# A long convolution's second half: joined loads, a filter that goes through DRAM, and loads five groups ahead

## The chip, the cores and the metric

The kernel runs on one core of a Trainium2 chip. The metric is the device time of one execution in microseconds. Before the change it is 1845.44 us, the median of 3 runs (1845.41 to 1846.05).

## What is computed

The reference has three parts. Only the first is touched by the change; the other two take most of the time.

```python
h_filt = (np.maximum(pos_emb @ w1, 0.0) @ w2) * window      # filter, 12480 x 128
u = x * v                                                  # signal, 12480 x 128
Uf = np.fft.rfft(u, n=2*S, axis=1); Hf = np.fft.rfft(h_filt, n=2*S, axis=0)
y = np.fft.irfft(Uf * Hf[None], n=2*S, axis=1)[:, :S]; attn = x * y
# then, on 12480 tokens of 128, with d_ff = 2048
h = t @ w_in; g = P(h) / (Q(h) + 1e-06); t = g @ w_out
h = t @ w_in2; g = where(h >= 1, h, where(h <= -1, 0, (h + 1)**2 / 4)); out = g @ w_out2
```

## The kernel before

The long transform (2 blocks x 128 x 49 points) is taken apart into a transform over n1 (128 points) and one over n2 (49 points). The function `conv_transform` does this in two halves, and then the two token layers run in a software pipeline of 49 tiles.

**First half** (lines 99 to 205): 14 chunks of the 49 columns m (`CHS`: 1, 2, eleven times 4, 2). For each chunk SyncE (SP) loads positions (`pt`), `x` and `v`; GpSimd (POOL) multiplies u = x*v; TensorE (PE) makes the filter's first layer and the transform over n1 (lines 193 to 195, six matrix products for each column). ScalarE (ACT) and VectorE (DVE) move the result out of PSUM: the signal parts into the tile `so`, which ACT's queue writes to the DRAM tensor `sd`, and the filter part into `sr`, a tile that stays in SBUF with one row of the transform (k1) on each partition. `so` has two buffers, `x` and `v` have three; loads are issued four chunks ahead.

**Second half** (lines 207 to 376): 34 groups of up to four values of k1 (first one group of 1, then 31 of 4, at the end two of 2). For a group the 98 values (49 columns, real and imaginary) have to lie on partitions. So `load` and `load_u` fetch `gt` (matrix of the transform over n2), `rr` (filter rows, four transfers out of `sr`, each from one partition of SBUF to 98) and `ru` (signal rows out of `sd`), all on SP's queue; `load_inv` fetches `gi`, the inverse matrix, at the step that runs. Then:

- `R`: transform of the filter rows on PE (line 244), split into a high and a low part by ACT (line 88) and DVE (line 89);
- `AB`: product with the second layer's weights on PE (lines 255 to 258), copied by ACT (line 260);
- `U`: transform of the signal on PE (line 269) into the PSUM tile `up`, which has one buffer;
- `M`: the spectral product, four operations on DVE (lines 286, 287, 289, 290) and four on POOL;
- `Tr` and `Inv`: transposes (line 306) and inverse transform (line 322) on PE with ACT copies, and the store of `co` into the DRAM tensor `cd` on ACT's queue.

Step s of the loop works on several groups at once: loads for s+3, AB for s+1, U and M for s, R for s+2, Tr for s-2, Inv for s-3. Beside it each step decodes a part of the layers' weights, which come as 64-bit floats: `fill` takes one of 32 fillers, each a load (line 57, two buffers), six operations on DVE (lines 68 to 71, 73, 74) and one or two on POOL, every second time one on ACT. The order is written out by hand, and every engine and SP's queue run in that order.

**After it** the layers' pipeline starts when the last part of `cd` has been written; its tiles load two columns of `cd` each (line 491).

Of the kernel before, what the change touches and what calls it, by code (L numbers as in the profile page):

```python
# [44 lines left out]
def decode_steps(nc, pool, src, n, dst):  # L45
    """float64 bits (src, int32 pairs low/high) to float32 in dst(), rounded to nearest:
    one closure per instruction."""
    e = {}

    def tile_(name, dt):  # L50
        e[name] = pool.tile([128, n], dt, name=name, tag=name, bufs=2 if name in "kt" else 1)
        return e[name]

    def load():
        e["b"] = pool.tile([128, n, 2], I32, name="b64", tag="b64", bufs=2)
        b = e["b"] if len(src.shape) == 3 else e["b"].rearrange("p (f d) t -> p f d t", f=src.shape[1])
        nc.sync.dma_start(b, src)

    def low():
        return e["b"][:, :, 0]  # L60

    def high():
        return e["b"][:, :, 1]

    ts, stt = nc.vector.tensor_scalar, nc.vector.scalar_tensor_tensor
    return [
        load,
        lambda: ts(tile_("t", I32), high(), 0x07FFFFFF, 3, op0=ALU.bitwise_and, op1=ALU.logical_shift_left),
        lambda: ts(tile_("a", I32), low(), 28, 1, op0=ALU.logical_shift_right, op1=ALU.bitwise_and),
        lambda: stt(e["t"], high(), -0x40000000, e["t"], op0=ALU.bitwise_and, op1=ALU.bitwise_or),  # L70
        lambda: stt(e["t"], low(), 29, e["t"], op0=ALU.logical_shift_right, op1=ALU.bitwise_or),
        lambda: nc.gpsimd.tensor_tensor(e["t"], e["t"], e["a"], op=ALU.add),
        lambda: ts(tile_("k", I32), high(), 27, 15, op0=ALU.logical_shift_right, op1=ALU.bitwise_and),
        lambda: stt(dst(), e["k"], 7.0, e["t"].bitcast(F32), op0=ALU.is_ge, op1=ALU.mult),
    ]


def conv_transform(tc, ident, io, cd, fillers, colsum):
    """Spectral product of u = x*v with the filter; leaves, per k1, the inverse
    transform over k2 in cd[k1, (block n2), re/im, d]."""  # L80
    nc = tc.nc
    xp, vp, posT, w1, w2, win, sgn, f1c, gc, gic = io
    with ExitStack() as ctx:
# [9 lines left out]
        sd = dram.tile([NK, N2, 2, 256], F32, name="sd")  # L93
        sr = big.tile([NK, N2, 2, D], F32, name="sr")
        w2h = big.tile([128, NB, D], F32R, name="w2h")
        w2l = big.tile([128, NB, D], F32R, name="w2l")
        rrg = pool("cv_rr", 1)

        # ---- filter MLP, u = x*v, transform over n1; block 1 takes block 0's
        # transform along, shifted by half a period  # L100
        with tc.tile_pool(name="ca", bufs=2) as ca, tc.tile_pool(name="cap", bufs=1, space=PSUM) as cap:
# [73 lines left out]
            for c in range(nch):  # L175
                if c + 4 < nch:
                    loads(c + 4)
                n = CHS[c]
                b = buf.pop(c)
                more = []  # L180
                if c + 1 < nch:
                    more += [lambda: parts(c + 1, 0)]
                if c + 2 < nch:
                    products(c + 2)
                    more += [lambda: mlp(c + 2)]
                if c + 1 < nch:
                    more += [lambda: parts(c + 1, 1)]
                so = ca.tile([NK, mx, 2, 256], F32, name="so", tag="so")
                for j in range(n):
                    sp = cap.tile([128, 2, 512], F32, name="sp", tag="sp", bufs=3)  # L190
                    for r in range(2):
                        o = sp[:, r, 0:SIG]
                        nc.tensor.matmul(o, f1h[:, r], b["h"][:, j], start=True, stop=False)
                        nc.tensor.matmul(o, f1l[:, r], b["h"][:, j], start=False, stop=False)
                        nc.tensor.matmul(o, f1h[:, r], b["l"][:, j], start=False, stop=True)
                    nc.scalar.copy(so[:, j, :, 0:128], sp[:, :, 0:128])
                    nc.scalar.copy(sr[:, first[c] + j], sp[:, :, 128:256])
                    nc.vector.scalar_tensor_tensor(so[:, j, :, 128:256], so[:, j, :, 0:128], sgt,
                                                   sp[:, :, 256:384], op0=ALU.mult, op1=ALU.add)
                    if more:  # L200
                        more.pop(0)()
                for fn in more:
                    fn()
                nc.scalar.dma_start(sd[:, first[c]:first[c] + n], so[:, 0:n])
            split(w2h, w2l, w2b)

        # ---- per k1: transform over n2, product, inverse transform over k2
# [4 lines left out]
        cdr = cd.rearrange("k (b m) r d -> (m r) k b d", b=NB)  # L212
        groups = [(NK, 1)] + [(4 * i, 4) for i in range(NK // 4 - 1)] + [(NK - 4, 2), (NK - 2, 2)]
        ng = len(groups)
        G = [dict() for _ in groups]

        def load(g):
            k0, n = groups[g]
            e = G[g]
            row = k0 % NK  # L220
            v, nb, m = ("n", 1, 1) if n == 1 else ("", 4, 4)
            e["rr"] = rrg.tile([SL, m, D], F32, name="rr", tag="rr" + v, bufs=nb)[:, 0:n]
            e["gt"] = rrg.tile([SL, m, SL], F32, name="gt", tag="gt" + v, bufs=nb)[:, 0:n]
            nc.sync.dma_start(e["gt"], gc[:, k0:k0 + n])
            for i in range(n):
                nc.sync.dma_start(e["rr"][:, i], sr[row + i:row + i + 1].rearrange("k m r s -> k (m r) s"))  # L226

        def load_u(g):
            k0, n = groups[g]
            row = k0 % NK  # L230
            G[g]["ru"] = (big if n == 1 else pre).tile([SL, n if n == 1 else 4, 256], F32, name="ru", tag=f"ru{min(n, 2)}", bufs=1 if n == 1 else 4)
            nc.sync.dma_start(G[g]["ru"][:, 0:n], sdr[:, row:row + n])

        def load_inv(g):
            k0, n = groups[g]
            G[g]["gi"] = (big if n == 1 else pre).tile([SL, n if n == 1 else 4, SL], F32, name="gi", tag=f"gi{min(n, 2)}", bufs=1 if n == 1 else 4)
            nc.sync.dma_start(G[g]["gi"][:, 0:n], gic[:, k0:k0 + n])

        def R(g):
# [3 lines left out]
            for i in range(n):  # L243
                nc.tensor.matmul(rp[:, i], e["rr"][:, i], e["gt"][:, i], start=True, stop=True)
# [17 lines left out]
        def U(g):  # L262
# [4 lines left out]
            for i in range(n):  # L267
                for b in range(NB):
                    nc.tensor.matmul(uv[:, i, b * SL:(b + 1) * SL], e["ru"][:, i, b * D:(b + 1) * D],
# [40 lines left out]
        def Inv(g, h):  # L310
# [13 lines left out]
            if h + 2 == n:  # L324
                for b in range(NB):
                    (nc.scalar if g < ng - TQ else nc.sync).dma_start(cdr[:, k0:k0 + n, b], e["co"][:, 0:n, b * D:(b + 1) * D])

        fills = fillers(pool("cv_fill", 1))
        late = []

        def fill(i):
            nonlocal late
            for fn in late:
                fn()
            late = []
            if i + 1 < len(fills):
                fills[i + 1][0]()
            if i < len(fills):
                for fn in fills[i][1:6]:
                    fn()  # L340
                late = fills[i][6:]

        for g in range(3):
            load(g)
        for g in range(3):
            load_u(g)
        fills[0][0]()
# [5 lines left out]
        for s in range(-2, ng + 3):  # L353
            if 3 <= s + 3 < ng:
                load(s + 3)
                load_u(s + 3)
            on(load_inv, s)
# [18 lines left out]
            fill(s + 2)  # L376
# [3 lines left out]
def kernel(ctx, tc, xp, vp, xT, posT, w1, w2, win, sgn, f1c, gc, gic, fic,  # L380
# [4 lines left out]
    cd = dram.tile([NK, NG, 2, D], F32, name="cd")  # L385
# [46 lines left out]
    # minus the column sums of w_out2, in parts  # L432
# [6 lines left out]
    with tc.manual_schedule():  # L439
        conv_transform(tc, ident, (xp, vp, posT, w1, w2, win, sgn, f1c, gc, gic), cd, fillers, colsum)  # L440
# [43 lines left out]
    # attention output of one token tile: inverse over k1, times x, split hi + lo  # L484
    def X0(t):
# [4 lines left out]
        ct = tok.tile([NK, TILES[t], 2, D], F32, name="ct", tag="ct", bufs=1)  # L490
        nc.sync.dma_start(ct, cd[:, c0 // 128:c0 // 128 + TILES[t]])
        x1[t] = {"x": xt, "c": ct}

    # its bank holds an accumulator too: emitted between two of its groups
    def XF(t):
        p = banks[XB_ACC][:, 256:256 + TILES[t] * 128]
        for j in range(TILES[t]):
            for r in range(2):
                nc.tensor.matmul(p[:, j * 128:(j + 1) * 128], x1[t]["c"][:, j, r], fit[:, r],
# [170 lines left out]
def constants():  # L670
# [11 lines left out]
    for s in range(NK + 1):  # L682
# [30 lines left out]
        "gc": np.ascontiguousarray(g.reshape(NK + 1, SL, SL).transpose(1, 0, 2).astype(f)),  # L713
        "gic": np.ascontiguousarray(gi.reshape(NK + 1, SL, SL).transpose(1, 0, 2).astype(f)),
# [4 lines left out]
def layout(inputs):  # L719
# [4 lines left out]
    def pad(v):  # L724
# [8 lines left out]
        "xT": x.reshape(NB, N1, N2, D).transpose(3, 0, 2, 1).reshape(D, COLS),  # L733
# [14 lines left out]
def unlayout(o):  # L748
    import numpy as np

    o = o.reshape(D, NB, N2, N1).transpose(1, 3, 2, 0).reshape(COLS, D)
# [19 lines left out]
```

## Time and profile before

| | |
|---|---|
| median of 3 runs | 1845.44 us |
| span of the profiled execution | 1846.1 us |
| PE busy | 1673.5 us (91%) |
| DVE busy | 1633.3 us (88%) |
| ACT busy | 1427.3 us (77%) |
| POOL busy | 1425.8 us (77%) |
| moved by DMA | 107.32 MB |
| HBM read, written | 66.98 MB, 32.11 MB |

The profiled execution spans 0.7 us more than the median of the runs. The page also cuts the span into 40 slices of 46 us, one digit for each, in tenths:

```profile
PE   6868878887789999999999999999999999999998
DVE  5647566773999999999999999999999999999994
PEclk9957888887999999999999999999999999999999
DMA  9756676772000000000000000000000000000000
```

The convolution is what stands in the first ten digits: the first half in the first two, the second half in the eight behind them. There the DMA engines are busy for 5 to 7 tenths, PE for 8, DVE for 5 to 7, and PE's granted clock is not full. From the tenth digit on come the layers, with DVE and PE at 9.

### The profile page before, as it was taken

The page shows a single profiled execution, that of the slowest core. Times are in us where ns is not written, and L with a number is a line of the kernel's source. Part 1 is how long each engine was busy: PE and PEld are TensorE (multiplying, and loading weights), DVE is VectorE, ACT ScalarE, POOL GpSimd, SP SyncE. Part 2 cuts the span into 40 slices and gives each one's busy share as a digit, 9 for nine tenths or more (in the row PEclk, how much of TensorE's full clock was granted, in tenths as well). Part 3 has the DMA queues.
Part 4 walks back from the last instruction along what each step waited for, and adds up shares of the span by engine and source line. Part 5 has one row for each costly group of instructions (what it writes and reads, how often), then busy time and mean ns, then how long its engine had stood idle before and what let it go on. Part 6 is the DMA issues. An engine that isn't in the chain of part 4 may idle for free.

```text
span 1846.1 us, 26908 instructions
## 1 busy us (share of the span) xinstructions
PE 1673.5 (91%) x10150; PEld 1508.6 (82%) x10150; DVE 1633.3 (88%) x1670; ACT 1427.3 (77%) x1737; POOL 1425.8 (77%) x858
## 2 busy tenths in 40 slices
PE   6868878887789999999999999999999999999998
PEld 6757767776688888888888888898888888888887
DVE  5647566773999999999999999999999999999994
ACT  4613333344799999999999999999999999999995
POOL 4335444554598899898898898998988998988996
PEclk9957888887999999999999999999999999999999
DMA  9756676772000000000000000000000000000000
GB/s 336 300 110 152 141 164 153 163 174 73 18 21 13 24 22 14 23 18 18 24 15 21 24 15 21 24 12 24 23 13 24 24 12 24 24 12 23 15 4 12
DMA packets 101660, 107.32 MB, mean 58 GB/s; under 512 B 8690, under 2 KB 84346, under 8 KB 100122
## 3 DMA queue, kind: packets, MB, share of 16 engines
q1 hardware_dynamic: 74514, 80.36, 17.1%
q10 hardware_dynamic: 26904, 25.11, 4.0%
q8 instruction: 80, 1.31, 0.3%
q14 instruction: 50, 0.41, 0.1%
q0 software_dynamic: 112, 0.13, 0.0%
HBM read 66.98 MB, written 32.11 MB: 54 GB/s over the span
## 4 chain that ended last, share of the span: by engine, by line
DVE 62%; DMA 14%; issue 12%; PE 6%; SPq 3%; ACT 2%; POOL 0%; DVEq 0%; ACTq 0%; POOLq 0%
DVE r L574 12%; DVE n L558 11%; DVE n L570 11%; DVE n L554 10%; DVE g L579 9%; DVE c L613 6%; DMA ru<-sd 5%; DMA rr<-sr 3%; DMA gi<-in_gic_dram 3%; SPq L226 2%; DMA sd<-so 2%; PE cp L322 1%; DVE o L645 1%; PE acc L482 1%; DVE xTt L504 1%
## 5 line engine op out<-in xcount | busy, mean ns | idle before, releaser
L635 POOL TENSOR_TENSOR y<-y,c 128x1024 f32<-128x1024 f32 x196 | 501.3, 2559 | 9.8 <-ACT c L629 3.8
L549 POOL TENSOR_TENSOR w<-w,z 128x1024 f32<-128x1024 f32 x196 | 468.7, 2391 | 16.3
L482 PE MATMUL acc<-g,wo 128*128 128x256 f32 x1568 | 382.4, 387 | 11.8 <-DVE g L579 8.7
L482 PE MATMUL acc<-y,wo 128*128 128x256 f32 x1568 | 370.5, 379 | 0.7 <-DVE o L645 0.7
L545 POOL TENSOR_SCALAR w<-z,ab 128x1024 f32<-128x1024 f32 x196 | 234.9, 1198 | 142.2 <-DVE r L574 89.0
L482 PEld LDWEIGHTS acc<-g,wo 128*128 128x128 f32 x1568 | 284.8, 191 | 51.6 <-DVE g L579 10.8
L482 PEld LDWEIGHTS acc<-y,wo 128*128 128x128 f32 x1568 | 283.6, 190 | 32.8 <-issue 1.0
L476 PE MATMUL h<-x2hi,hi 128*128 128x256 f32 x784 | 252.6, 322 | 55.2 <-DVE n L558 52.4
L476 PE MATMUL h<-x1hi,hi 128*128 128x256 f32 x784 | 256.7, 327 | 9.4 <-ACT y L618 5.0
L618 ACT ACTIVATE y<-h 128x1024 f32<-128x1024 f32 x196 | 200.8, 1025 | 83.0 <-PE h L478 82.9
L554 DVE SCALAR_TENSOR_TENSOR n<-f,co,h 128x1024 f32<-128x1024 f32 x196 | 248.6, 1268 | 6.7 <-ACT f L536 6.7
L570 DVE SCALAR_TENSOR_TENSOR n<-n,co,r 128x1024 f32<-128x1024 f32 x196 | 248.8, 1270 | 4.6 <-ACT r L566 4.6
L558 DVE SCALAR_TENSOR_TENSOR n<-n,co,h 128x1024 f32<-128x1024 f32 x196 | 248.1, 1266 | 0.0
L574 DVE SCALAR_TENSOR_TENSOR r<-w,r 128x1024 f32<-128x1024 f32 x196 | 238.3, 1216 | 0.0
L579 DVE SCALAR_TENSOR_TENSOR g<-r,n 128x1024 f32<-128x1024 f32 x196 | 237.3, 1211 | 0.1
L566 ACT ACTIVATE r<-L 128x1024 f32<-128x1024 f32 x196 | 201.3, 1027 | 44.1 <-DVE g L579 43.0
L478 PE MATMUL h<-x1lo,hi 128*128 128x256 f32 x784 | 222.2, 283 | 0.0
L477 PE MATMUL h<-x1hi,lo 128*128 128x256 f32 x784 | 222.0, 283 | 0.0
L478 PE MATMUL h<-x2lo,hi 128*128 128x256 f32 x784 | 221.8, 283 | 0.0
L477 PE MATMUL h<-x2hi,lo 128*128 128x256 f32 x784 | 221.5, 283 | 0.0
L476 PEld LDWEIGHTS h<-x2hi,hi 128*128 128x128 f32 x784 | 149.1, 190 | 86.7 <-DVE n L558 81.6
L562 ACT ACTIVATE L<-w 128x1024 f32<-128x1024 f32 x196 | 208.6, 1064 | 0.0
(94 smaller groups left out, 3353.4 us busy)
## 6 DMA issues: line engine op xcount, KB each, us to landing
ct<-cd SPq DMA_DIRECT2D x49, 256.0 KB
ru<-sd SPq DMA_DIRECT2D x31, 392.0 KB
cd<-co ACTq DMA_DIRECT2D x60, 196.0 KB
sd<-so ACTq DMA_DIRECT2D x11, 1024.0 KB
rr<-sr SPq DMA_DIRECT2D x129, 49.0 KB
xTt<-in_xT_dram SPq DMA_DIRECT2D x49, 128.0 KB
out_dram<-o SPq DMA_DIRECT2D x49, 128.0 KB
xt<-in_xp_dram SPq DMA_DIRECT2D x11, 512.0 KB
```

The lines of the kernel that those rows point to most:

```text
L476: nc.tensor.matmul(o, hi[:, f], x[0], start=True, stop=False)
L477: nc.tensor.matmul(o, lo[:, f], x[0], start=False, stop=False)
L478: nc.tensor.matmul(o, hi[:, f], x[1], start=False, stop=True)
L482: nc.tensor.matmul(ps, W[l][2][:, f], g[:, k * w:(k + 1) * w], start=f == 0, stop=f == NF - 1)
L545: nc.gpsimd.tensor_scalar(s["w"], s["z"], ab[:, 1:2], ab[:, 0:1], op0=ALU.mult, op1=ALU.add)
L549: nc.gpsimd.tensor_tensor(s["w"], s["w"], s["z"], op=ALU.mult)
L554: nc.vector.scalar_tensor_tensor(s["n"], s["f"], a[2], s["h"], op0=ALU.add, op1=ALU.mult)
L558: nc.vector.scalar_tensor_tensor(s["n"], s["n"], a[1], s["h"], op0=ALU.add, op1=ALU.mult)
L570: nc.vector.scalar_tensor_tensor(s["n"], s["n"], a[0], s["r"], op0=ALU.add, op1=ALU.mult)
L574: nc.vector.scalar_tensor_tensor(s["r"], s["w"], 1.000001, s["r"], op0=ALU.add, op1=ALU.mult)
L579: nc.vector.scalar_tensor_tensor(s["g"], s["r"], 2.0, s["n"], op0=ALU.subtract, op1=ALU.mult, reverse0=True)
L635: nc.gpsimd.tensor_tensor(s["y"], s["y"], s["c"], op=ALU.add)
```

## The change

- `sd` gets 384 columns in place of 256: the filter rows go to DRAM beside the signal rows. ACT copies both out of PSUM in one operation, and `sr` is gone.
- `load` fetches a group's filter and signal rows with one transfer (`ru`, rows of 1,536 bytes), six buffers.
- The two matrices stand in one array `ggc`, and `load_g` fetches both with one transfer (`gg`), nine buffers.
- Loads are issued five groups ahead. The first five `gg` and the first two decode loads are issued in the first half, behind chunk 10.
- Decode loads run two fillers ahead with three buffers. Two fillers stand before the loop and two in each of the first two steps, so the 32 fillers end four steps earlier.
- `cd` has rows of 256 elements (both blocks), so a group's result goes out in one transfer with pieces of 1 KB. The token order of `xT` and of the output follows; a tile's loads keep their sizes.

```diff
-        sd = dram.tile([NK, N2, 2, 256], F32, name="sd")
-        sr = big.tile([NK, N2, 2, D], F32, name="sr")
+        sd = dram.tile([NK, N2, 2, SIG], F32, name="sd")
...
+        def load_g(g):
+            k0, n = groups[g]
+            t = ggp.tile([SL, 1 if n == 1 else 4, 2, SL], F32, name="gg", tag="ggn" if n == 1 else "gg",
+                         bufs=1 if n == 1 else 9)
+            nc.sync.dma_start(t[:, 0:n], ggc[:, k0:k0 + n])
+            G[g]["gt"], G[g]["gi"] = t[:, 0:n, 0], t[:, 0:n, 1]
...
-                    nc.scalar.copy(so[:, j, :, 0:128], sp[:, :, 0:128])
-                    nc.scalar.copy(sr[:, first[c] + j], sp[:, :, 128:256])
+                    nc.scalar.copy(so[:, j, :, 0:256], sp[:, :, 0:256])
...
+                if c == nch - 4:
+                    for g in range(5):
+                        load_g(g)
+                    fill_load(0)
+                    fill_load(1)
...
-            nc.sync.dma_start(e["gt"], gc[:, k0:k0 + n])
-            for i in range(n):
-                nc.sync.dma_start(e["rr"][:, i], sr[row + i:row + i + 1].rearrange("k m r s -> k (m r) s"))
+            t = pre.tile([SL, 1 if n == 1 else 4, SIG], F32, name="ru", tag="run" if n == 1 else "ru",
+                         bufs=1 if n == 1 else 6)
+            nc.sync.dma_start(t[:, 0:n], sdr[:, row:row + n])
...
-                for b in range(NB):
-                    (nc.scalar if g < ng - TQ else nc.sync).dma_start(cdr[:, k0:k0 + n, b], e["co"][:, 0:n, b * D:(b + 1) * D])
+                (nc.scalar if g < ng - TQ else nc.sync).dma_start(cdr[:, k0:k0 + n], e["co"][:, 0:n])
...
-        for g in range(3):
+        for g in range(5):
             load(g)
-        for g in range(3):
-            load_u(g)
-        fills[0][0]()
+        for i in range(2):
+            fill(i)
+        done = 2
...
-            if 3 <= s + 3 < ng:
-                load(s + 3)
-                load_u(s + 3)
-            on(load_inv, s)
+            if 5 <= s + 5 < ng:
+                load(s + 5)
+                load_g(s + 5)
...
-            fill(s + 2)
+            for i in range(2 if s < 0 else 1):
+                fill(done)
+                done += 1
```

SP's queue in a step of the second half before; `b` is the decode load, and x4 says that four such transfers follow each other:

```order
L224 DMA gt<-in_gc_dram 98x392
L226 DMA rr<-sr 98x1x128 x4
L232 DMA ru<-sd 98x4x256
L237 DMA gi<-in_gic_dram 98x392
L57 DMA b_1284<-in_w_in_dram 128x512
```

The same queue now, two steps:

```order
L249 DMA ru<-sd 98x4x384
L122 DMA gg<-in_ggc_dram 98x784
L57 DMA b_1186<-in_w_in_dram 128x512
L249 DMA ru<-sd 98x4x384
L122 DMA gg<-in_ggc_dram 98x784
L57 DMA b_1258<-in_w_out_dram 128x2x256
```

Of eight transfers in a step three are left; no transfer goes from SBUF to SBUF any more.

DVE at the start of the second half before, from the first split of a filter group (line 89) to the first spectral product (line 286); lines 68 to 74 decode:

```order
L89 TENSOR_TENSOR rs_978<-rp_975,rs_977 128x98
L68 TENSOR_SCALAR t<-b_973 128x256
L69 TENSOR_SCALAR a<-b_973 128x256
L70 SCALAR_TENSOR_TENSOR t<-b_973,t 128x256
L71 SCALAR_TENSOR_TENSOR t<-b_973,t 128x256
L89 TENSOR_TENSOR rs_1005<-rp_999,rs_1004 128x392
L73 TENSOR_SCALAR k<-b_973 128x256
L74 SCALAR_TENSOR_TENSOR w_1010<-k,t 128x256
L68 TENSOR_SCALAR t<-b_981 128x256
```

And now, between the same two splits:

```order
L89 TENSOR_TENSOR rs_950<-rp_947,rs_949 128x98
L73 TENSOR_SCALAR k<-b_784 128x256
L74 SCALAR_TENSOR_TENSOR wo_75<-k,t 128x256
L68 TENSOR_SCALAR t<-b_923 128x256
L69 TENSOR_SCALAR a<-b_923 128x256
L70 SCALAR_TENSOR_TENSOR t<-b_923,t 128x256
L71 SCALAR_TENSOR_TENSOR t<-b_923,t 128x256
L73 TENSOR_SCALAR k<-b_923 128x256
L74 SCALAR_TENSOR_TENSOR w_967<-k,t 128x256
L68 TENSOR_SCALAR t<-b_938 128x256
L69 TENSOR_SCALAR a<-b_938 128x256
L70 SCALAR_TENSOR_TENSOR t<-b_938,t 128x256
```

Fillers 0 and 1 stand ahead of the first split now but for the end of filler 1, and two fillers stand between each two splits of the start where one stood. The third decode load (b_923) is issued on SP behind the five `ru` loads.

## Rows read from the trace of the kernel before

**Rows 1.** Windows: start:end, length, PE, PEld, DVE, ACT, POOL busy, clock, DMA, GB/s

```profile
140.00:370.00 230.00, 189.68 (x1047) 163.07 (x1045) 150.85 (x253) 82.97 (x148) 113.74 (x127) 0.83 0.69 155
```

**Rows 2.** The chain that ended last from 150 to 400, by line

```profile
by line: DMA ru<-sd 33.0%; DMA rr<-sr 21.0%; DMA gi<-in_gic_dram 20.9%; SPq L226 8.3%; PE cp L322 6.6%; PE tp L306 2.3%; PE rp L244 1.6%; PE up L269 1.4%; issue 1.0%; PE ap L255 0.9%; PE ap L256 0.8%; PE ap L258 0.7%; DVE m L287 0.7%; DVE m
```

**Rows 3.** Windows of 1 us, in the `rr` transfers and behind them

```profile
308.00:309.00 1.00, 1.00 (x11) 1.00 (x11) 0.53 (x2) 0.00 (x0) 0.00 (x0) 1.00 0.48 26
...
313.00:314.00 1.00, 0.42 (x2) 0.43 (x3) 0.00 (x0) 0.00 (x0) 0.51 (x1) 0.50 0.99 331
```

**Rows 4.** Timeline of SP's queue: start, length, engine, line, transfer

```profile
302.92 3.89 SPq L226 DMA_DIRECT2D rr<-sr  x4
306.85 0.68 SPq L232 DMA_DIRECT2D ru<-sd  x1
```

**Rows 5.** Timeline of DVE: first operation of M; idle before, releaser in brackets

```profile
116.87 0.25 DVE L286 TENSOR_TENSOR m<-up,ab 128x98 f32<-128x98 f32 x1
...
139.78 0.57 DVE L286 TENSOR_TENSOR m<-up,ab 128x392 f32<-128x392 f32 x1 [0.47 <-PE up L269]
...
263.44 0.57 DVE L286 TENSOR_TENSOR m<-up,ab 128x392 f32<-128x392 f32 x1 [3.90 <-PE up L269]
...
270.50 0.56 DVE L286 TENSOR_TENSOR m<-up,ab 128x392 f32<-128x392 f32 x1
...
283.97 0.57 DVE L286 TENSOR_TENSOR m<-up,ab 128x392 f32<-128x392 f32 x1 [3.87 <-PE up L269]
...
291.45 0.55 DVE L286 TENSOR_TENSOR m<-up,ab 128x392 f32<-128x392 f32 x1
...
400.11 0.57 DVE L286 TENSOR_TENSOR m<-up,ab 128x392 f32<-128x392 f32 x1 [3.53 <-PE up L269]
...
407.17 0.56 DVE L286 TENSOR_TENSOR m<-up,ab 128x392 f32<-128x392 f32 x1
...
413.93 0.57 DVE L286 TENSOR_TENSOR m<-up,ab 128x392 f32<-128x392 f32 x1 [1.70 <-PE up L269]
```

**Rows 6.** Timeline of DVE: where the decode begins in one step

```profile
266.63 0.79 DVE L73 TENSOR_SCALAR k<-b 128x256 int32<-128x256 int32 x1
```

**Rows 7.** Timeline of PE: a slow inverse transform, and one step without a wait

```profile
276.32 3.62 PE L322 MATMUL cp<-zt,gi 98*98 98x256 f32 x8
...
281.94 1.93 PE L269 MATMUL up<-gt,ru 98*128 98x98 f32 x16
...
285.03 1.89 PE L322 MATMUL cp<-zt,gi 98*98 98x256 f32 x8
...
288.27 1.93 PE L269 MATMUL up<-gt,ru 98*128 98x98 f32 x16
```

**Rows 8.** DMA from 20 to 62, in the first half

```profile
DMA packets 6729, 17.00 MB, mean 405 GB/s; under 512 B 504, under 2 KB 560, under 8 KB 6074
```

**Rows 9.** Timeline of ACT's queue: the `sd` stores of chunks 2, 8 and 13

```profile
27.87 0.33 ACTq L204 DMA_DIRECT2D sd<-so  x1
...
66.55 0.33 ACTq L204 DMA_DIRECT2D sd<-so  x1
...
90.22 0.33 ACTq L204 DMA_DIRECT2D sd<-so  x1
```

**Rows 10.** Timeline of DVE at the start of the second half

```profile
112.33 0.29 DVE L68 TENSOR_SCALAR t<-b 128x256 int32<-128x256 int32 x1 [16.20 <-DMA b<-in_w_in_dram]
```

**Rows 11.** DMA queues from 200 to 400: packets, MB, share of 16 engines

```profile
q1 hardware_dynamic: 25909, 23.64, 55.7%
q10 hardware_dynamic: 16341, 8.08, 13.8%
```

**Rows 12.** Operations on the decode tile `b`, 150 to 420: count, ns min/median/max

```profile
L73 DVE TENSOR_SCALAR k<-b x27: 281/927/1008, 152.4 to 410.1; 128x256 int32<-128x256 int32 x27
L68 DVE TENSOR_SCALAR t<-b x26: 279/296/1133, 154.2 to 405.1; 128x256 int32<-128x256 int32 x26
```

**Rows 13.** Window at the start of the second half

```profile
120.00:140.00 20.00, 18.16 (x88) 16.83 (x87) 15.49 (x26) 4.57 (x8) 10.74 (x12) 0.64 0.65 120
```

More of the change, by code (lines that the diff above doesn't have):

```diff
@@ L54, in load @@
     def load():
-        e["b"] = pool.tile([128, n, 2], I32, name="b64", tag="b64", bufs=2)
+        e["b"] = pool.tile([128, n, 2], I32, name="b64", tag="b64", bufs=3)
         b = e["b"] if len(src.shape) == 3 else e["b"].rearrange("p (f d) t -> p f d t", f=src.shape[1])
@@ L81, in conv_transform @@
     nc = tc.nc
-    xp, vp, posT, w1, w2, win, sgn, f1c, gc, gic = io
+    xp, vp, posT, w1, w2, win, sgn, f1c, ggc = io
     with ExitStack() as ctx:
@@ L92, in conv_transform, with fill_load, fill @@
         dram = pool("cv_dram", 1, space=bass.MemoryType.DRAM)
-        sd = dram.tile([NK, N2, 2, 256], F32, name="sd")
-        sr = big.tile([NK, N2, 2, D], F32, name="sr")
+        sd = dram.tile([NK, N2, 2, SIG], F32, name="sd")
         w2h = big.tile([128, NB, D], F32R, name="w2h")
         w2l = big.tile([128, NB, D], F32R, name="w2l")
-        rrg = pool("cv_rr", 1)
+        ggp = pool("cv_gg", 1)
+        groups = [(NK, 1)] + [(4 * i, 4) for i in range(NK // 4 - 1)] + [(NK - 4, 2), (NK - 2, 2)]
+        ng = len(groups)
+        G = [dict() for _ in groups]
+        fills = fillers(pool("cv_fill", 1))
+        late = []
+        def fill_load(i):
+            if i < len(fills):
+                fills[i][0]()
+        def fill(i):
+            nonlocal late
+            for fn in late:
+                fn()
+            late = []
+            fill_load(i + 2)
+            if i < len(fills):
+                for fn in fills[i][1:6]:
+                    fn()
+                late = fills[i][6:]
+        def load_g(g):
[4 more added lines that the diff above has]
+            G[g]["gt"], G[g]["gi"] = t[:, 0:n, 0], t[:, 0:n, 1]
         with tc.tile_pool(name="ca", bufs=2) as ca, tc.tile_pool(name="cap", bufs=1, space=PSUM) as cap:
@@ L187, in conv_transform @@
                     more += [lambda: parts(c + 1, 1)]
-                so = ca.tile([NK, mx, 2, 256], F32, name="so", tag="so")
+                so = ca.tile([NK, mx, 2, SIG], F32, name="so", tag="so")
                 for j in range(n):
@@ L195, in conv_transform @@
                         nc.tensor.matmul(o, f1h[:, r], b["l"][:, j], start=False, stop=True)
-                    nc.scalar.copy(so[:, j, :, 0:128], sp[:, :, 0:128])
-                    nc.scalar.copy(sr[:, first[c] + j], sp[:, :, 128:256])
-                    nc.vector.scalar_tensor_tensor(so[:, j, :, 128:256], so[:, j, :, 0:128], sgt,
+                    nc.scalar.copy(so[:, j, :, 0:256], sp[:, :, 0:256])
+                    nc.vector.scalar_tensor_tensor(so[:, j, :, 256:384], so[:, j, :, 0:128], sgt,
                                                    sp[:, :, 256:384], op0=ALU.mult, op1=ALU.add)
@@ L211, in conv_transform @@
         sdr = sd.rearrange("k m r s -> (m r) k s")
[L212 to L215, printed above, removed]
+        cdr = cd.rearrange("k m r s -> (m r) k s")
         def load(g):
             k0, n = groups[g]
-            e = G[g]
             row = k0 % NK
-            v, nb, m = ("n", 1, 1) if n == 1 else ("", 4, 4)
-            e["rr"] = rrg.tile([SL, m, D], F32, name="rr", tag="rr" + v, bufs=nb)[:, 0:n]
-            e["gt"] = rrg.tile([SL, m, SL], F32, name="gt", tag="gt" + v, bufs=nb)[:, 0:n]
-            nc.sync.dma_start(e["gt"], gc[:, k0:k0 + n])
-            for i in range(n):
-                nc.sync.dma_start(e["rr"][:, i], sr[row + i:row + i + 1].rearrange("k m r s -> k (m r) s"))
[L228 to L237, printed above, removed]
+            t = pre.tile([SL, 1 if n == 1 else 4, SIG], F32, name="ru", tag="run" if n == 1 else "ru",
+                         bufs=1 if n == 1 else 6)
+            nc.sync.dma_start(t[:, 0:n], sdr[:, row:row + n])
+            G[g]["ru"] = t
         def R(g):
@@ L243, in R @@
             for i in range(n):
-                nc.tensor.matmul(rp[:, i], e["rr"][:, i], e["gt"][:, i], start=True, stop=True)
+                nc.tensor.matmul(rp[:, i], e["ru"][:, i, D:2 * D], e["gt"][:, i], start=True, stop=True)
             e["rs"] = [grp.tile([128, 4, SL], F32R, name=f"rs{k}", tag=f"rs{k}", bufs=2) for k in range(2)]
@@ L268, in U @@
                 for b in range(NB):
-                    nc.tensor.matmul(uv[:, i, b * SL:(b + 1) * SL], e["ru"][:, i, b * D:(b + 1) * D],
+                    nc.tensor.matmul(uv[:, i, b * SL:(b + 1) * SL], e["ru"][:, i, 2 * b * D:(2 * b + 1) * D],
                                      e["gt"][:, i], start=True, stop=True)
@@ L324, in Inv @@
             if h + 2 == n:
-                for b in range(NB):
-                    (nc.scalar if g < ng - TQ else nc.sync).dma_start(cdr[:, k0:k0 + n, b], e["co"][:, 0:n, b * D:(b + 1) * D])
[L328 to L341, printed above, removed]
-        for g in range(3):
+                (nc.scalar if g < ng - TQ else nc.sync).dma_start(cdr[:, k0:k0 + n], e["co"][:, 0:n])
+        for g in range(5):
             load(g)
-        for g in range(3):
-            load_u(g)
-        fills[0][0]()
+        for i in range(2):
+            fill(i)
+        done = 2
         def on(fn, g, *a):
@@ L375, in conv_transform, with kernel @@
                     colsum(cs, part, 4)
-            fill(s + 2)
+            for i in range(2 if s < 0 else 1):
+                fill(done)
+                done += 1
 @with_exitstack
-def kernel(ctx, tc, xp, vp, xT, posT, w1, w2, win, sgn, f1c, gc, gic, fic,
+def kernel(ctx, tc, xp, vp, xT, posT, w1, w2, win, sgn, f1c, ggc, fic,
                           w_in1, w_out1, ca, cb, w_in2, w_out2, out):
@@ L384 @@
     dram = ctx.enter_context(tc.tile_pool(name="dram", bufs=1, space=bass.MemoryType.DRAM))
-    cd = dram.tile([NK, NG, 2, D], F32, name="cd")
+    cd = dram.tile([NK, N2, 2, NB * D], F32, name="cd")
     cp = ctx.enter_context(tc.tile_pool(name="const", bufs=1))
@@ L439 @@
     with tc.manual_schedule():
-        conv_transform(tc, ident, (xp, vp, posT, w1, w2, win, sgn, f1c, gc, gic), cd, fillers, colsum)
+        conv_transform(tc, ident, (xp, vp, posT, w1, w2, win, sgn, f1c, ggc), cd, fillers, colsum)
     nc.scalar.activation(ab, co[:, 4:6], AF.Abs)
@@ L489, in X0 @@
         nc.sync.dma_start(xt, xT[:, c0:c0 + w])
-        ct = tok.tile([NK, TILES[t], 2, D], F32, name="ct", tag="ct", bufs=1)
-        nc.sync.dma_start(ct, cd[:, c0 // 128:c0 // 128 + TILES[t]])
+        ct = tok.tile([NK, TILES[t] // NB, 2, NB * D], F32, name="ct", tag="ct", bufs=1)
+        nc.sync.dma_start(ct, cd[:, c0 // 256:c0 // 256 + TILES[t] // NB])
         x1[t] = {"x": xt, "c": ct}
@@ L498, in XF @@
             for r in range(2):
-                nc.tensor.matmul(p[:, j * 128:(j + 1) * 128], x1[t]["c"][:, j, r], fit[:, r],
+                nc.tensor.matmul(p[:, j * 128:(j + 1) * 128], x1[t]["c"][:, j // NB, r, j % NB * D:(j % NB + 1) * D], fit[:, r],
                                  start=r == 0, stop=r == 1)
@@ L712, in constants @@
         "f1c": f1.astype(f),
-        "gc": np.ascontiguousarray(g.reshape(NK + 1, SL, SL).transpose(1, 0, 2).astype(f)),
-        "gic": np.ascontiguousarray(gi.reshape(NK + 1, SL, SL).transpose(1, 0, 2).astype(f)),
+        "ggc": np.ascontiguousarray(np.stack([g.reshape(NK + 1, SL, SL), gi.reshape(NK + 1, SL, SL)], 1)
+                                    .transpose(2, 0, 1, 3).astype(f)),
         "fic": fi.astype(f),
@@ L732, in layout @@
         "vp": v,
-        "xT": x.reshape(NB, N1, N2, D).transpose(3, 0, 2, 1).reshape(D, COLS),
+        "xT": x.reshape(NB, N1, N2, D).transpose(3, 2, 0, 1).reshape(D, COLS),
         "posT": pos.reshape(NB, N1, N2, 64).transpose(0, 3, 2, 1).reshape(128, N2, N1),
@@ L749, in unlayout @@
     import numpy as np
-    o = o.reshape(D, NB, N2, N1).transpose(1, 3, 2, 0).reshape(COLS, D)
+    o = o.reshape(D, N2, NB, N1).transpose(2, 3, 1, 0).reshape(COLS, D)
     return np.ascontiguousarray(o[:SEQ])
```

## Prediction

> **What bounds the kernel now.** I read the page's 40 slices first: the change touches only the convolution, the first 440 us or so, and what comes behind it keeps its loads' sizes and its order. Then I took the second half as one window. From 140 to 370 PE is busy for 190 of 230 us and DVE for 151, at a mean granted clock of 0.83, and the DMA engines for 0.69 of it at only 155 GB/s [rows 1]. No engine is full, so something passes between them. The chain of waits names it: three quarters of 150 to 400 are `ru`, `rr` and `gi` transfers [rows 2]. They stand on one queue, so the chain steps from one to the next; which of them is slow is told by windows of 1 us. While the four `rr` transfers run, the engines move 26 GB/s; behind them, with `ru`, the decode load and the stores, 331 GB/s [rows 3]. The 196 KB of `rr` come out of single partitions of SBUF, and SP spends 3.9 us issuing them [rows 4]. So a step is some 5 us of slow `rr` and some 5 us of all else, in turn.
>
> The last view is the first DVE operation of M, which marks each step. Groups 3 and 31 stand at 139.78 and 413.93 [rows 5]: 28 full steps in 274.2 us, 9.79 us each. They are not even. After a long step the next one sometimes finds its rows there: 263.44 to 270.50, 283.97 to 291.45 and 400.11 to 407.17, that is 7.06, 7.48 and 7.06 us, and at the end of each DVE shows no idle time before M [rows 5]. So these three are steps at DVE's own pace. In the first of them the decode takes 266.63 to 270.50, 3.9 of 7.1 us [rows 6].
>
> **The change part by part.**
>
> *Steps with a decode.* Once rows and matrices lie ready, the step is set by the slowest engine. DVE keeps all its operations: the mean of the three steps is 7.20 us. PE keeps its operations too: from one U to the next without a wait it needs 281.94 to 288.27, 6.33 us [rows 7], hidden under DVE. The `rr` transfers that go cost the difference to 9.79. Does DMA hide? A group moves 588 KB (`ru`), 300 (`gg`) and 256 (`b`) on SP's queue and 392 on ACT's, in all the same 1,536 KB as before. From 200 to 400 SP's queue took 55.7% of 16 engines for 23.64 MB, 75.4 engine-us for one MB, and ACT's 13.8% for 8.08 MB, 54.7 [rows 11]. At these old prices, with the slow `rr` in them, 1.17 MB and 0.40 MB are 88 and 22 engine-us, 6.9 us on 16 engines. That is under 7.2, and the new pieces are longer; so I cost DMA at nothing. Of the step's eight issues on SP three are left, of ACT's two one. Six and nine buffers put a load's landing some three steps ahead of its use, so no wait takes the place of the one for `rr`; without that cover it would be the 6.9 us above, still no loss.
>
> The fillers end four steps earlier: decodes fill steps up to group 26, and behind it PE's 6.33 sets the pace. From group 3 to group 31: 23 x 7.20 + 5 x 6.33 = 165.6 + 31.7 = 197.3 us, 76.9 less than 274.2.
>
> A place where the skill bears on it: two decode operations on DVE are uneven, 281 ns at least and 927 in the median for line 73, 279 and up to 1133 for line 68 [rows 12], and they run beside POOL's products. The Trainium skill, "SBUF — State Buffer", section "SBUF: two separate sides", says that DVE and GpSimd share a port pair under an exclusive lock, so that the loser waits for the whole instruction. The steps of 7.06 us bear that out and hold one such wait each; a denser order could add more, which is a rival below.
>
> *First half.* The `sd` stores grow by half, 49 columns x 128 KB = 6.4 MB. The engines move 405 GB/s there between 20 and 62 [rows 8], so 6.4 MB are 16 us if all of it lies on the path: the upper end. Chunks 2 to 8 store at 27.87 to 66.55, 6.45 us each, then loads are over, and the last five come by 90.22 at the pace of the engines [rows 9]. A full chunk moves 2,304 KB now (2.36 MB, 5.8 us at 405) and 2,816 KB after (2.88 MB, 7.1 us). Six chunks longer by 0.65 (bare bandwidth) to 1.45 us (7.1 x 6.45 / 5.8) are 4 to 9 us; behind them DMA has room for what is left and for the 1.8 MB of early loads. One ACT copy in place of two can give back up to 3 us where ACT is late. Bounds -3 to +16; I take +6, the nearest row being the chunk's own pace.
>
> *Start of the second half.* From the last store to the first M it is 90.22 to 116.87 [rows 5, 9], 26.7 us, and DVE waits in it until 112.33 for the first decode load, which stands behind nine `rr` and three `ru` [rows 10]. Now the third decode load stands behind five `ru`, 2.5 MB, 6.3 us at 405, all waiting for the last store. With 2 to 3 us for that store and as much for the load's own way that is 11 to 12 us after the store's issue. Then DVE has the rest of two steps with two decodes each, 4 x 3.9 at most, 3 x 3.9 if filler 5 is half behind M: about 12 us. Together 23 to 24. I take 3.5 less than before; bounds -12 (the decodes hidden) to +4 (loads slower). The decodes are not added work: they are those that end earlier.
>
> *Groups 0 to 3.* 22.9 us before [rows 5], set by DVE and by PE at a mean clock of 0.64 [rows 13]. The early loads change neither, 0 (bounds -2 to +3). Behind group 31 the work is what it was, but for one issue less: 0.
>
> Sum, against the span of 1846.1 us: +6 - 3.5 - 76.9 = -74.4, so 1771.7; the runs' median is 0.7 lower: **1771 us**. With the parts' likely spread (first half +4 to +10, the step 7.06 to 7.48) the likeliest case has 1764 to 1785.
>
> **The rivals.**
>
> *The first half pays in full and the start gives nothing back.* For it: the DMA engines are at their limit up to 62 [rows 8], and the second half's first load now waits for the stores. Against: behind 62 there is room. +16 and 0 in place of +6 and -3.5: 1784 us. Chance 0.13.
>
> *The lock stretches DVE's step.* For it: line 73's median is near its maximum [rows 12], and POOL's 114 us in 230 [rows 1] come to 4.8 us of each step, packed closer in 7.2 than in 9.8. Against: the three quick steps hold the same POOL work. If lines 68 and 73 both ran at their maxima (1133 and 1008 in place of 296 and 927), 0.9 us more a step: 23 x 0.9 = 21, so 1792 us. Chance 0.10.
>
> *Transfers still set the pace.* For it: 6.9 us at old prices is close. If only the mean of 155 GB/s of before rose by what the faster windows show without `rr`, to about 200, 1.57 MB would be 7.9 us a step: 23 x 0.7 + 5 x 1.5 = 24, so 1795. Against: 331 GB/s in such a window. Chance 0.06. In the Trainium skill, "DMA: Bandwidth & Descriptors", section "Why a DMA increments its semaphore by 16 and not by 1", a transfer runs on the largest number up to 16 of engines that divides its rows, so 98 rows run on 14; by that alone the 6.9 above would be about 7.7 us and the time about 1790, an estimate from that page.
>
> *PE stays at the slower of its two clock levels.* This one is slower. It is granted 0.64 at the start of the second half [rows 13] and falls when PE waits for `rr`: the inverse transform at 276.32 takes 3.62 us for the 1.89 us of the one at 285.03 [rows 7]. At 1.2 GHz PE needs up to 2 x 6.33 = 12.7 us a step, and 28 steps are 355 us in place of 274: some 1924 us. It decides from the point where the 28 steps are slow by 2.7 us over the forecast's mean of 7.0, which is about half of them held at the lower level. Against: the step from 281.94 to 288.27 ran at the full level of 2.4 GHz [rows 7], and with rows at hand PE waits under 1 us in 7.2. Chance 0.04.
>
> **How the numbers follow.** The forecast 0.67, the rivals 0.13, 0.10, 0.06 and 0.04. The range reaches over the first three rivals and, below, over a start that hides its decodes: 1760 to 1798. About 0.2% (3.7 us) is what a measurement of this kernel can tell from no change: faster 0.95, within it 0.01, slower 0.04.
>
> **What would show it.** In the changed kernel's profile: no transfer from SBUF to SBUF; the last `sd` store near 96 us; the first M near 119; full groups 7.2 us apart with hardly any idle time of DVE before M, 6.3 behind group 26; clock near 1 from the fifth group on; group 31 near 340 in place of 414. Wrong it would be if PE waited for `ru` or `gg` within a step, if full groups stood over 8 us apart, or if the first M came behind 130.

## The result and the profile after

The changed kernel takes 1784.59 us, the median of 4 runs (1780.26 to 1786.96); its ratio to the kernel before is 0.9651, with an interval of 0.9626 to 0.9675. The profiled execution spans 1785.2 us; it is the slowest of the four. Forecast were 1771 us, in 1760 to 1798. All numbers here are of runs at the usual granted clock; one run of e4 took 2730.02 us at a mean clock of 0.586 and is left out.

The second half in one window (columns as in [rows 1]); the last line is one of 4 us in which row loads and, behind them, decode loads are under way:

```profile
140.00:330.00 190.00, 170.57 (x1163) 151.54 (x1163) 183.64 (x282) 90.03 (x161) 131.17 (x142) 0.97 0.73 204
...
116.00:120.00 4.00, 1.59 (x8) 1.34 (x7) 0.00 (x0) 0.00 (x0) 0.00 (x0) 0.50 1.04 257
```

DVE is busy for 184 of 190 us where it was busy for two thirds, and PE's granted clock is 0.97 where it was 0.83. The chain from 150 to 320 (its end is cut off here) has no transfer at its head any more:

```profile
by line: PE up L282 11.9%; DVE m L300 10.9%; DVE m L303 10.9%; DVE t L68 7.4%; DVE m L299 6.9%; PE rp L257 6.3%; DVE rs L89 5.9%; DVE m L302 5.8%; DVE k L73 5.5%; DVE w L74 5.3%; DVE a L69 4.3%; PE tp L319 3.9%; PE ap L271 3.7%; issue 3.1%;
```

The first DVE operation of M marks the steps as in [rows 5]: groups 0, 3, 7 to 9, 26 to 28 and 31.

```profile
132.90 0.25 DVE L299 TENSOR_TENSOR m<-up,ab 128x98 f32<-128x98 f32 x1
...
153.49 0.56 DVE L299 TENSOR_TENSOR m<-up,ab 128x392 f32<-128x392 f32 x1
...
184.45 0.56 DVE L299 TENSOR_TENSOR m<-up,ab 128x392 f32<-128x392 f32 x1
192.03 0.56 DVE L299 TENSOR_TENSOR m<-up,ab 128x392 f32<-128x392 f32 x1
199.06 0.56 DVE L299 TENSOR_TENSOR m<-up,ab 128x392 f32<-128x392 f32 x1
...
323.61 0.56 DVE L299 TENSOR_TENSOR m<-up,ab 128x392 f32<-128x392 f32 x1
329.85 0.57 DVE L299 TENSOR_TENSOR m<-up,ab 128x392 f32<-128x392 f32 x1 [1.17 <-PE up L282]
336.18 0.57 DVE L299 TENSOR_TENSOR m<-up,ab 128x392 f32<-128x392 f32 x1 [3.05 <-PE up L282]
...
354.74 0.57 DVE L299 TENSOR_TENSOR m<-up,ab 128x392 f32<-128x392 f32 x1 [2.84 <-PE up L282]
```

Steps with a decode are 7.58 and 7.03 us in turn, without idle time of DVE; behind group 26 they are 6.24 to 6.33 us, the last one 5.91, and DVE waits for PE. Group 31 stands 59.2 us earlier than before. But group 0 stands 16.0 us later [rows 5]: what the steps gained, the way to them gave back in part. ACT's queue shows where: the stores of chunks 7, 8 and 13; for the last two compare [rows 9].

```profile
66.19 0.33 ACTq L229 DMA_DIRECT2D sd<-so  x1
78.87 0.33 ACTq L229 DMA_DIRECT2D sd<-so  x1
...
105.70 0.33 ACTq L229 DMA_DIRECT2D sd<-so  x1
```

The last store comes at 105.70 where it came at 90.22. Between chunks 7 and 8 lie 12.7 us; there the early matrix loads run, on SP's queue from 69.67, and PE stands still:

```profile
69.67 7.43 SPq L122 DMA_DIRECT2D gg<-in_ggc_dram  x5
```

```profile
75.00:80.00 5.00, 0.00 (x0) 0.00 (x0) 0.09 (x1) 0.71 (x2) 0.07 (x1) 1.00 0.92 239
```

ACT waits there too. Its first copy behind the store of chunk 8 shows what the profile puts the wait down to: not a store, but the last load of `v`, which was issued at 68.87, just ahead of the matrix loads, and was under way for 9.9 us.

```profile
79.29 0.58 ACT L222 COPY so<-sp 128x512 f32<-128x512 f32 x1 [7.98 <-DMA vt<-in_vp_dram]
```

### The profile page after: what moved, and what is told of

The parts are those of the page before. It is cut to its first block, busy times and chain, and to the rows that moved or that the text cites. A ratio compares the mean times of both kernels' runs of the same rounds, so it can differ in the third digit from the quotient of the medians.

```text
span 1785.2 us, 26590 instructions
## 1 busy us (share of the span) xinstructions
PE 1631.3 (91%) x10150; PEld 1479.1 (83%) x10150; DVE 1641.9 (92%) x1670; ACT 1424.0 (80%) x1688; POOL 1428.2 (80%) x858
## 4 chain that ended last, share of the span: by engine, by line
DVE 72%; issue 12%; PE 8%; DMA 5%; ACT 1%; POOL 1%; SPq 0%; DVEq 0%; POOLq 0%; ACTq 0%
DVE r L572 12%; DVE n L556 11%; DVE n L568 11%; DVE n L552 10%; DVE g L577 10%; DVE c L611 6%; DMA sd<-so 3%; PE up L282 2%; DVE m L300 1%; DVE m L303 1%; DMA vt<-in_vp_dram 1%; PE cp L335 1%; DVE o L643 1%; PE acc L480 1%; DVE xTt L502 1%
## 5 line engine op out<-in xcount | busy, mean ns | idle before, releaser
L564 ACT ACTIVATE r<-L 128x1024 f32<-128x1024 f32 x196 | 201.3, 1027 | 44.5 <-DVE g L577 43.4
```

## The experiments

Theory: the transfers out of single SBUF partitions held the steps, and their going is the whole gain; the first half pays for the bytes of the wider store, for the early loads among them and for the store buffers; the start pays for four decodes behind the row loads. Rivals: joining and the five groups ahead are needed for the gain; and, for the loss, the bytes alone. Of two executions with the same first half (the changed kernel and e4) the last store stood at 105.70 and 104.05; in e6, where the same early bytes come in ten matrix loads in place of five, it stood at 102.33. So a difference of 2 to 3 us there tells nothing by itself.

**e1: early matrix loads on another queue, later.**

```diff
-        def load_g(g):
+        def load_g(g, queue=None):
...
-            nc.sync.dma_start(t[:, 0:n], ggc[:, k0:k0 + n])
+            (queue or nc.sync).dma_start(t[:, 0:n], ggc[:, k0:k0 + n])
...
-                        load_g(g)
+                        load_g(g, nc.scalar)
```

> The changed kernel with one edit: the five early matrix loads go on ACT's queue behind the store of chunk 10 instead of SP's queue, where they start at 69.7. Theory A (they collide with the stores of chunks 7 and 8 while DMA is full): the last sd store comes at about 100 instead of 105.7, the time falls by 4 to 7 us to about 1779. Rival B (only the bytes of the wider stores count, and all of them lie on the path): the last store stays at 105 to 106 and the time at 1783 to 1786.

1783.57 us (1781.94 to 1787.15), last store at 101.97, first M at 130.13. Between the two: the store moved by 3.7, the median by only 1.0, which is inside the spread. What the edit does show is the gap: chunks 7 and 8 store at 65.47 and 71.53, 6.1 us apart for 12.7, so the early loads had made it. Behind chunk 10 the loads then held up ACT itself (4.4 us of issue, a wait of 5.8 us), so part of their price is only moved. What they cost in time is not settled by this run; e7 and e8 take it up.

**e2: a third store buffer.**

```diff
-                so = ca.tile([NK, mx, 2, SIG], F32, name="so", tag="so")
+                so = ca.tile([NK, mx, 2, SIG], F32, name="so", tag="so", bufs=3)
```

> The changed kernel with one edit: the tile so has three buffers instead of two. Theory A (ACT waits 24 us for a store buffer to come free, and that wait is what the wider store costs): the last store at 97 to 100, the time 1777 to 1780. Rival B (bandwidth: DMA is full until 75 anyway): ACT's waits move to the loads, the last store at 103 to 106, the time within 3 us of 1784.6.

1779.90 us (1777.53 to 1781.29), last store at 101.33, first M at 128.15. The time, 4.7 us less, lies in theory A's range; the store lies between the two theories. ACT's waits for a store fell, by the table of waits (24.1 us in six waits before the edit):

```profile
ACT so L222 <- DMA sd<-so: 6.0, 1, 6.0
```

One long wait stayed, ahead of the store of chunk 8, and grew from 8.0 to 12.8 us; the profile puts it down to a `gg` load. The buffers are a part of the loss and not all of it.

**e3: the wider store's bytes alone, in the kernel before.**

```diff
+        sx = dram.tile([NK, N2, 2, D], F32, name="sx")
...
+                nc.scalar.dma_start(sx[:, first[c]:first[c] + n], sr[:, first[c]:first[c] + n])
                 nc.scalar.dma_start(sd[:, first[c]:first[c] + n], so[:, 0:n])
```

> The kernel before with one part of the change alone: the filter rows are also stored to a DRAM tensor that nothing reads (6.4 MB more), one more store for each chunk ahead of the sd store; all else as before. If bandwidth is what counts: the last store 11 to 16 us later than 90.2, the time 1856 to 1862. If the room behind the loads takes most of it up: under 6 us later, 1847 to 1851.

1858.31 us in one run, 12 above the kernel before; the last store at 97.67, 7.5 us later than 90.22. By the store this is half of the rival "all bytes on the path", and near the +6 of the forecast; by its time the run lies in that rival's range, and the 4 us beyond the store are not explained. The bytes go here in a store of their own, from another tile. e5 has the wider store itself and comes to the same 7.8 us, so some 8 of the 15.5 us that the changed kernel lost there are not bytes.

**e4: no fillers in the first two steps.**

```diff
-            for i in range(2 if s < 0 else 1):
+            for i in range(0 if s < 0 else 1):
```

> The changed kernel with one edit: no fillers in the first two steps of the second half, so four of them run four steps later. Theory A (DVE, waiting for a decode load behind the five row loads and then working off four decodes, sets the first M at 132.9): first M at about 120, full steps with a decode four more at 7.3 instead of 6.33 (+4), the time 1774 to 1778. Rival B (the row loads set the start): first M not before 128, the time 1784 to 1788.

1777.48 us (1773.79 to 1777.54), ratio 0.9614 (0.9588 to 0.9640), 7 less. The first M stands at 119.67 and now waits for PE, no longer for decodes:

```profile
119.67 0.26 DVE L299 TENSOR_TENSOR m<-up,ab 128x98 f32<-128x98 f32 x1 [2.62 <-PE up L282]
```

In the changed kernel DVE waits at this place for the third decode load, then works off the decodes:

```profile
123.07 0.29 DVE L68 TENSOR_SCALAR t<-b 128x256 int32<-128x256 int32 x1 [8.19 <-DMA b<-in_w_in_dram]
```

Theory A holds, in the first M and in the time.

**e5: the filter through DRAM alone, in the kernel before.** Loads stay three ahead and apart, as before.

```diff
-                    nc.scalar.copy(sr[:, first[c] + j], sp[:, :, 128:256])
+                    nc.scalar.copy(so[:, j, :, 256:384], sp[:, :, 128:256])
...
-            for i in range(n):
-                nc.sync.dma_start(e["rr"][:, i], sr[row + i:row + i + 1].rearrange("k m r s -> k (m r) s"))
+            nc.sync.dma_start(e["rr"], sdr[:, row:row + n, 256:384])
```

(`sd` and `so` get 384 columns, and `ru` is loaded from the first 256.)

> The kernel before with one part of the change alone: the filter rows go to DRAM in the sd store and come back with one rr transfer for each group; the matrices, ru, cd and the decode loads stay apart and three groups ahead, as before. Theory A (the transfers out of single SBUF partitions are all that held the steps): full steps with a decode at 7.2 to 7.5 us from about the fifth group on, PE without waits for rr, the last store 7 to 12 us later than 90.2, the time 1780 to 1793. Rival B (joined loads or five groups ahead are needed as well): full steps still at 8.3 us or more, the time 1810 or more.

1775.77 us (1773.01 to 1778.14), ratio 0.9615 (0.9591 to 0.9640): all of the gain and 8.8 us more than the whole change, and below the range of theory A. Its second half, the window of [rows 1], and two of its steps:

```profile
140.00:370.00 230.00, 203.38 (x1411) 179.17 (x1409) 205.36 (x319) 110.91 (x200) 150.25 (x166) 0.99 0.72 197
```

```profile
177.52 0.56 DVE L284 TENSOR_TENSOR m<-up,ab 128x392 f32<-128x392 f32 x1
184.55 0.56 DVE L284 TENSOR_TENSOR m<-up,ab 128x392 f32<-128x392 f32 x1
192.13 0.56 DVE L284 TENSOR_TENSOR m<-up,ab 128x392 f32<-128x392 f32 x1
```

7.03 and 7.58 us, as in the changed kernel, with seven transfers a step for four. The last store is at 97.98, as in e3. Rival B is out. The edit takes the source out of SBUF and makes one transfer of four; which of the two made the four slow is not separated here.

**e6: the joined transfers apart again.**

```diff
-            nc.sync.dma_start(t[:, 0:n], ggc[:, k0:k0 + n])
+            for r in range(2):
+                nc.sync.dma_start(t[:, 0:n, r], ggc[:, k0:k0 + n, r])
...
-                (nc.scalar if g < ng - TQ else nc.sync).dma_start(cdr[:, k0:k0 + n], e["co"][:, 0:n])
+                for b in range(NB):
+                    (nc.scalar if g < ng - TQ else nc.sync).dma_start(
+                        cdr[:, k0:k0 + n, b * D:(b + 1) * D], e["co"][:, 0:n, b * D:(b + 1) * D])
```

> The changed kernel with the joined transfers taken apart again: the two matrices in two loads, the result in two stores of 512-byte pieces. Theory A (DMA is hidden under DVE's step): steps stay at 7.3, the time within 4 us of 1784.6. Rival B (joining pays): the two more issues and the shorter pieces bring waits into the steps, 0.3 us a step or more, 1794 or more.

1783.30 us (1781.48 to 1785.16): no difference. DMA is busier, and hidden all the same; here 170 to 310 of e6 and of the changed kernel:

```profile
170.00:310.00 140.00, 126.15 (x884) 111.67 (x883) 137.36 (x211) 70.63 (x126) 97.56 (x106) 1.00 0.87 218
```

```profile
170.00:310.00 140.00, 127.22 (x890) 112.79 (x889) 137.37 (x211) 70.69 (x127) 96.78 (x105) 1.00 0.78 216
```

**e7: three groups ahead.**

```diff
-                    for g in range(5):
+                    for g in range(3):
...
-            if 5 <= s + 5 < ng:
-                load(s + 5)
-                load_g(s + 5)
+            if 3 <= s + 3 < ng:
+                load(s + 3)
+                load_g(s + 3)
```

(and three loads ahead of the loop.)

> The changed kernel with loads three groups ahead instead of five (three early matrix loads). Theory A (a landing well under a step is ahead enough): steps stay at 7.3; two fewer row loads and matrices stand before the third decode load, so the start is 3 to 6 us shorter: 1778 to 1784. Rival B (five ahead is needed): PE waits for ru or gg within steps, some 1 us a step, 1800 or more.

1775.75 us (1775.70 to 1778.83), 8.8 less: more than theory A had. Steps stay at 7.31; the last store is at 100.87 and the first M at 124.64, 8.3 us earlier. The two farther groups brought nothing, and 3.4 us of the 8.3 lie behind the last store, where two row loads fewer stand ahead of the decode load; the 4.8 us of the store are little more than its scatter, but the gap between chunks 7 and 8 is 8.9 us for 12.7.

**e8: the edits together** (three store buffers, no fillers in the first two steps, matrices of groups 3 and 4 behind the row loads).

> The changed kernel with three edits: three so buffers, no fillers in the first two steps of the second half, and the matrices of groups 3 and 4 loaded behind the row loads instead of in the first half. If the first half's store buffers and the start's decodes cost what the single edits showed (4.7 and 7 us): last store at 99 to 101, first M at 114 to 117, the time 1769 to 1774. If the two gains overlap (a store that lands earlier only lengthens another wait): 1775 to 1778.

1772.23 us (1769.87 to 1773.92), ratio 0.9592 (0.9572 to 0.9612). Last store at 97.28, first M at 113.12, both 1 to 2 us earlier than forecast: the gains add up (4.7 and 7.1 us in e2 and e4, 12.4 here).

**e9: e7 with e2's and e4's edits.**

> The changed kernel with loads three groups ahead, three so buffers, and no fillers in the first two steps of the second half. If the early matrix loads still cost something in the five-ahead version with the same two other edits (1772.2): last store at 95 to 97, first M at 111 to 113, the time 1768 to 1771. If not: 1771 to 1774.

1771.62 us (1768.93 to 1774.13), last store at 97.83, first M at 113.82. Not told apart from e8: the time lies in the second case's range, and the store and the first M come 0.8 us behind the first's, so fewer loads ahead give nothing more here. Both have the lowest medians of all, some 13 us under the changed kernel.

**e10: e5 with e2's edit.**

> The kernel before with the filter rows through DRAM alone and a third so buffer. Theory: the store buffers hold the first half while DMA is full and not after it, so the last store comes 1 to 4 us earlier than 98.0 and the time falls by as much from 1775.8: 1772 to 1775. Rival: the first half's end is at DMA's pace there, no change: 1775 to 1777.

1773.78 us (1770.69 to 1774.93) and 97.03 for 97.98: 2.0 in the medians with ranges that overlap, 1.0 at the last store. The buffer is worth little where no early loads run among the stores, as against 4.7 in e2.

## Why the prediction was near, and which step was off

The span fell by 60.9 us for the 74.4 of the sum. Of the 13.5 us between them the first half has 9.5, the start 4.0 and the steps 4.0; groups 0 to 3 (2.3) and what lies behind group 31 (1.7) went the other way.

*The steps* came out as worked out: DVE's own pace at first, PE's 6.33 behind group 26. From group 3 to 31 it is 153.49 to 354.74, 201.3 us for the forecast's 197.3. DVE's step is 7.31 in the mean for 7.20, and one early step, from 161.07, took 8.75: PE's granted clock was 0.50 from 160 to 165. The two lengths come from line 69: behind a line 68 of 1.13 us it takes 0.28 or 0.82 us, in turn. Here are two steps in a row of the changed kernel, on DVE:

```profile
182.41 1.12 DVE L68 TENSOR_SCALAR t<-b 128x256 int32<-128x256 int32 x1
183.46 0.28 DVE L69 TENSOR_SCALAR a<-b 128x256 int32<-128x256 int32 x1
...
189.45 1.13 DVE L68 TENSOR_SCALAR t<-b 128x256 int32<-128x256 int32 x1
190.50 0.82 DVE L69 TENSOR_SCALAR a<-b 128x256 int32<-128x256 int32 x1
```

Line 68 now stands near its old maximum in every step (median 1130 ns for 296 in [rows 12]), and line 73 at 792 for 927. So the rival of the port lock was right that decodes wait more than in the median of before, and wrong in the price: 0.1 us a step, not 0.9. The quick steps had held these waits already, and more than the one each that the prediction read in them; in the step from 263.44 line 73 took 0.79 us, line 74 1.01 and line 68 1.12:

```profile
268.46 1.12 DVE L68 TENSOR_SCALAR t<-b 128x256 int32<-128x256 int32 x1
```

So most of the rival's 0.9 us stood in the 7.20 from the start. That POOL's operations are what they wait for is inferred from their place in time and was not tested.

*DMA at nothing* holds in the steps: e5 and e6 show that joining and piece sizes change no step. The rival at 1795, and the estimate of about 1790 beside it, are out: the engines' share is 0.78 while the steps run at DVE's pace.

*The first half* is the step that failed, in its size: +15.5 us for the +6 taken, at the edge of its bounds. The number for the bytes was near (e3 +7.5, e5 +7.8). What was wrong is that behind chunk 8 DMA "has room" for the 1.8 MB of early loads. They do not wait for that room. They start as soon as SP's queue reaches them, while the engines are still full, and chunk 8's store then stands at 78.87 for 66.55, in e5 at 71.98. Its wait is not for a store buffer, since the copies into its tile were done at 71.3; by the profile it is for a load that is under way beside the early ones, and why a store waits for that load stays open. Behind it ACT waits for store buffers again. The last store's issue in us, by early matrix loads and store buffers:

| early matrix loads | two buffers | three buffers |
|---|---|---|
| five | 105.70, 104.05; 102.33 in e6 | 101.33 (e2) |
| three | 100.87 (e7) | 97.28 (e8), 97.83 (e9) |
| one `gt` alone, no early decode load | 97.98 (e5) | 97.03 (e10) |

So with two buffers five early matrix loads cost 4 to 8 us and three cost 3, and a third buffer takes back nearly all of it where three are early. The last row's kernels also copy out of PSUM in two ACT operations for one, and each place but two holds one execution with a scatter of up to 3 us; a finer division between loads and buffers stays open.

*The start* was forecast 3.5 us shorter and is 27.2, 0.5 longer. Its decodes took 9.8 (123.07 to 132.90) for some 12. But the first row load was issued at 110.33, 4.6 us behind the last store's issue, for the 2 to 3 us taken, a term that no row of before shows; and row and decode loads took from there until 123.07, 12.7 for the 8 to 9 worked out from 405 GB/s. The window from 116 to 120 above shows why: full engines, 257 GB/s. A rate of the first half's transfers was used for row loads of 1,536-byte pieces; whether the size of the pieces makes the difference was not tested.

*Groups 0 to 3* took 20.6 for 22.9. The rival that gave 1784 hit the number, and both of its terms (+16 and 0 for +15.5 and +0.5), partly by luck: its 16 us were to be bytes, and bytes are half of it, while the 4 us that the steps took more were made up elsewhere. One of the prediction's own signs of being wrong came true, the first M behind 130 (132.90); the last store near 96 and group 31 near 340 were missed as well (105.70, 354.74). And its likeliest case is stated too wide: the two spreads that it names, -2 to +4 us and 23 steps of 0.14 less to 0.28 more, give 1766 to 1781, not 1764 to 1785.

## What to carry to other kernels

When a profile shows a slow kind of transfer on the path, replace that one first and measure it alone: here it was all of the gain, and the joined loads and the greater distance that came with it brought nothing. A load issued early is not free because a later stretch has room: it runs where its queue reaches it, so ask what it runs beside and whose buffers wait there. Work moved ahead of a loop's first step is on the path there, even if the engine that does it is idle on average.

## What the runs showed of the hardware

- Transfers out of one SBUF partition moved 26 GB/s with DMA at 0.48 [rows 3]; the same rows out of DRAM, in one transfer for four, fell out of the chain (e5).
- At an engine share of 1.04 both times the rate was 405 GB/s in the first half (from 20 to 62 before) [rows 8] and 257 while row loads of 1,536-byte pieces and decode loads ran at the second half's start. Which property of the transfers makes the difference was not tested.
- PE's granted clock went from 0.83 to 0.97 and 0.99 in the second half once waits for rows were gone; no edit aimed at it.
